# Gated gradient times w2 transposed made ahead of each chunk's MLP, w1 transposed kept on chip, third chunk turned on TensorE

## The chip, the cores and the metric

The kernel runs on one core of one Trainium2 chip. The metric is device time in microseconds (us) of one execution; the time of a kernel is the median of several executions. Of one execution there is also a hardware profile. Its engines are PE (TensorE, matrix products), PEld (the loads of PE's weights), DVE (VectorE), ACT (ScalarE), POOL (GpSimd) and SP (SyncE, which here only issues DMAs). Each engine works through its own instructions in the order in which the program wrote them; all engines run at once and wait for each other by semaphores. ACT and POOL issue some DMAs too, in the same order as their other instructions.

## The reference

The forward pass of one transformer block with adaptive layer norms, and the gradients of all its inputs. It is differentiated with `jax.vjp`, so the kernel computes both the output and nine gradients.

```python
mod = (silu(c) @ w_mod).reshape(1, 6, 1, 512)
sa, ca, ga, sb, cb, gb = (mod[:, i] for i in range(6))
h = layernorm(x) * (1 + ca) + sa
x = x + ga * attention(h, wqkv, wo)        # 32 heads of 16, 2048 tokens
h = layernorm(x) * (1 + cb) + sb
x = x + gb * (relu(h @ w1 + b1) ** 2 @ w2 + b2)   # 512 -> 1792 -> 512
```

For this change only the MLP's backward matters. With g the incoming gradient, gf = gb * g (the gated gradient), z = h @ w1 + b1, r = relu(z) and s = r * r, it needs ds = gf @ w2^T, then dz = 2 * r * ds, then dh = dz @ w1^T, and the weight gradients s^T @ gf (for w2) and h^T @ dz (for w1). All inputs and outputs are bf16.

## The kernel before

2048 tokens are four chunks of 512. The program has five stages, one after the other: a preparation (norms, first projections); the forward attention; the last chunk's MLP; the backward attention; and a tail.

**Forward attention.** 512 units of work, one for a chunk of queries (4), a group of four heads (8) and a tile of 128 keys (16). In each unit PE makes the scores of four heads (`psST`, L579), ACT takes their exponential in two instructions (`ET`, L581), and PE multiplies the result of two units earlier with the values (L595). The pool of `psST` has three buffers of two heads, so PE's scores can be up to one and a half units ahead of ACT.

**Dense work in the forward.** While the attention of chunk c+1 runs, the dense work of chunk c (the output projection, the second norm, the MLP forward and backward, the gradient up to the attention) is cut into steps, and `step` (L1128) puts one step into each unit. `dense_chunk` (L321) is a generator that yields after each step; `yield n` waits n units, `yield -2` runs one weight-gradient product ("chain", four products of 128 tokens each, `add_chain` L225) out of the queue `dwq`. All these steps use one PSUM bank (`pm`, one buffer), so a step's product waits until DVE has emptied the one before. `later(lag, ...)` puts an instruction, mostly a DMA on SP's queue, `lag` units later.

For one chunk, in order: O_c turned by a DMA transpose (L343), projection, norm, xn2 turned by a DMA transpose (L365), then 14 products z = w1^T h (L404, tile `wA`), each followed on DVE by the relu into `rT` (L406) and the square into `sT` (L407); then w2 transposed is loaded into the same buffer `wA` (L412), and 14 products ds (L418) follow, each multiplied on DVE by 2 r into dz (L421). Then dh (L444) with w1 transposed out of `wB`, which each chunk loads again from a copy in DRAM (`w1T_st`, L295); then the MLP's output (L500) and the attention gradient (`attn_grad`, L528). gf is made on POOL (L306) and turned by a DMA.

**The last chunk** cannot hide behind forward attention. `late_finish` (L659) and `last_chunk` (L1245) run it alone, on PE with all engines free for it. It loads w2 transposed and w1 transposed (L1529 to L1534), finishes the norm while PE runs chains left over from chunk 2 (`fill`, L1287 and L1295), and then has two loops of 14 iterations, each with a `tick` that issues what is due and then runs one chain:

- first loop (L1344): product z; relu on ACT (L1349); square on DVE (L1350); tick; `turn` of the s of the iteration before: four PE transposes (L1334) and a copy on ACT (L1335);
- second loop (L1359): product ds (L1362); dz on DVE straight out of PSUM (L1365); tick; `turn` of the dz of the iteration before.

A chain of the last chunk adds what earlier chunks left in DRAM: DVE adds `acc` and the fetched part (L236), and at the next tick ACT issues the DMA of the result (L237). Because ACT's queue is in order, ACT waits there until DVE has made the result. After the loops come dh (L1388), the layer-norm gradient, the attention gradient and the MLP's output (L1440), with the loads for the backward attention in between (`head_loads`; K as `KS_tok`, L1373; dOs as `dOs_tok`, L1475).

Of the kernel before, what the change touches and what calls it, by code (L numbers as in the profile page):

```python
# [13 lines left out]
dt = mybir.dt  # L14
# [6 lines left out]
P = 128  # L21
D = 512
DC = 4
# [11 lines left out]
def kernel(  # L35
# [64 lines left out]
    w1T_st = dram.tile([P, FC, D], BF, name="w1T_st")  # L100
# [45 lines left out]
    with ExitStack() as ph:  # L146
# [32 lines left out]
        def later(lag, f, *args):  # L179
            due.append((unit[0] + lag, f, args))  # L180

        def run_due(everything=False):
            i = 0
            while i < len(due):
                if everything or due[i][0] <= unit[0]:
                    _, f, args = due.pop(i)
                    f(*args)
                else:
                    i += 1
# [88 lines left out]
        def load_wB(src, lag, rate=1):  # L278
            w = ffw.tile([P, FC, D], BF, name="wB", tag="wB")
            for s in range(7):  # L280
                later(lag + int(s * rate), sp, w[:, 2 * s:2 * s + 2, :], src[:, 2 * s:2 * s + 2, :])
            return w

# [3 lines left out]
        begun = {}  # L287

        def chunk_loads(c):
            ts = slice(4 * c, 4 * c + 4)  # L290
            end = c == QC - 1
            if end:
                L = dict(begun)
            else:
                L = {"w1": load_wA(w1_src, 6), "w1T": load_wB(w1T_st[:], 20)}  # L295
                L["g"] = cb.tile([P, 4, D], BF, name="g_c", tag="g_c")
                sp(L["g"][:], g_dram[:, ts, :])
            L["wo"] = ffw.tile([P, DC, D], BF, name="wo_nat", tag="wo")
            sp(L["wo"][:], A_wo.rearrange("(oc p) j -> p oc j", p=P))
            L["x1"] = cb.tile([P, 4, D], BF, name="x1_c", tag="x1_c")  # L300
            sp(L["x1"][:], x_dram[:, ts, :])
            L["gf"] = cb.tile([P, 4, D], BF, name="gf_c", tag="gf")
            L["gfT"] = cb.tile([P, 4, DC, P], BF, name="gfT", tag="gfT")

            def scaled(ti):
                POOL.tensor_tensor(L["gf"][:, ti, :], L["g"][:, ti, :], gb_bc, ALU.mult)  # L306
                if ti < 3:
                    return
                later(3, sp, L["gfT"].rearrange("p t o q -> p (t o) q"), flat(L["gf"]), True)

            def sums(ti):
                rowsum(4, L["g"][:, ti, :], 4 * c + ti)

            if end:
                return L
            for ti in range(4):
                later(14 + ti, scaled, ti)
                later(27 + 2 * ti, sums, ti)
            return L

        def dense_chunk(c, O_c, L):  # L321
            ts = slice(4 * c, 4 * c + 4)
            g_c, x1_c, gf_c, gfT, w1_nat, w1T = (L[key] for key in ("g", "x1", "gf", "gfT", "w1", "w1T"))
# [19 lines left out]
            later(3, sp, OT.rearrange("p t o q -> p (t o) q"), flat(O_c), True)  # L343
            yield 6
# [11 lines left out]
            stats(2)  # L356
            stats(3)
# [5 lines left out]
            for ti in range(4):  # L363
                normed(ti)
            later(3, sp, h2T.rearrange("p t o q -> p (t o) q"), flat(xn2_c), True)  # L365
            yield 6
            while dwq and dwq[0][1] < c:
                yield -2
            for ic in range(DC):
# [12 lines left out]
            rT = cb.tile([P, FC, 512], BF, name="rT", tag="rT")  # L382
# [18 lines left out]
            for fc in range(FC):  # L401
# [4 lines left out]
                DVE.tensor_scalar(rT[:, fc, :], pz[:], b1col[:, fc:fc + 1], 0.0, ALU.add, ALU.max)  # L406
                DVE.tensor_tensor(sT[:, fc, :], rT[:, fc, :], rT[:, fc, :], ALU.mult)  # L407
# [4 lines left out]
            w2T = load_wA(w2T_st[:], 1)  # L412
            yield 3
            dzT = rT
            for fc in range(FC):
                pds = mm()
                for oc in range(DC):
                    PE.matmul(pds[:], w2T[:, oc, fc * P:(fc + 1) * P], gfT[:, :, oc, :],  # L418
                              start=(oc == 0), stop=(oc == DC - 1))
                db1p = wk.tile([P, 1], F32, name="db1p", tag="db1p")  # L420
                DVE.scalar_tensor_tensor(out=dzT[:, fc, :], in0=pds[:], scalar=2.0, in1=rT[:, fc, :],  # L421
                                         op0=ALU.mult, op1=ALU.mult, accum_out=db1p[:])
                POOL.tensor_tensor(db1acc[:, fc:fc + 1], db1acc[:, fc:fc + 1], db1p[:], ALU.add)
                yield 0
                if fc % 3 == 2 or fc == FC - 1:
                    f0 = fc // 3 * 3
                    while len(dwq) > FC - (fc + 1) + n_dz[0]:
                        yield -2
                    to_tokens("dz", dzT, f0, fc + 1)
            if c == QC - 2:  # L430
                begun["w1"] = load_wA(w1_src, 1)
            else:
                w2_nat = ffw.tile([P, FC, D], BF, name="w2_nat", tag="wA")
                for s in range(7):
                    later(1 + 3 * s, sp, w2_nat[:, 2 * s:2 * s + 2, :], w2_src[:, 2 * s:2 * s + 2, :])
# [4 lines left out]
            for ti in range(4):  # L440
                t = 4 * c + ti
                pdh = mm()
# [48 lines left out]
            if c == QC - 2:  # L491
                w2_nat = load_wB(w2_src, 1)
                yield 6
            else:
                yield 3
# [17 lines left out]
            later(2, sp, out0_v[:, ts, :], x1_c[:])  # L513
            if c == QC - 2:
                begun["g"] = cb.tile([P, 4, D], BF, name="g_c", tag="g_c")
                later(1, sp, begun["g"][:], g_dram[:, 4 * c + 4:4 * c + 8, :])
            dOs_c = cb.tile([P, 4, D], BF, name="dOs_c", tag="xn2_c")
            dOT = cb.tile([P, DC, 4, P], BF, name="dOT", tag="gfT")
# [114 lines left out]
        def early_finish():  # L633
# [8 lines left out]
            gf, gl = L["gf"], L["g"]  # L642
            for ti in range(4):
                later(1 + ti // 2, scale_heads, O_c, ou, ti, 4 * qc + ti, g)
                later(3 + ti // 2, DVE.tensor_tensor, gf[:, ti, :], gl[:, ti, :], gb_bc, ALU.mult)
# [33 lines left out]
        def ffinish(qc, rr, ou, L):  # L679
# [5 lines left out]
            for ti in range(4):  # L685
                scale_heads(O_c, ou, ti, qc * 4 + ti, HG)
            dense.append(dense_chunk(qc, O_c, L))
# [43 lines left out]
        def turn_weights(i):  # L731
            if i == 2:
                turned["1"] = ffw.tile([P, FC, D], BF, name="w1T_0", tag="wB")
                turned["2"] = ffw.tile([P, DC, FF], BF, name="w2T_0", tag="wA")
                turned["o"] = ffw.tile([P, DC, D], BF, name="woT_0", tag="wo")
            if 2 <= i < 6:
                for fc in range(4 * (i - 2), min(FC, 4 * (i - 2) + 4)):
                    sp(turned["1"][:, fc, :], B_w1[:, fc * P:(fc + 1) * P], True)
            if 7 <= i < 11:
                sp(turned["2"][:, i - 7, :], B_w2[:, (i - 7) * P:(i - 6) * P], True)  # L740
                sp(turned["o"][:, i - 7, :], A_wo[:, (i - 7) * P:(i - 6) * P], True)
            if i == 12:
                sp(w1T_st[:], turned["1"][:])
# [382 lines left out]
        loads = {}  # L1126

        def step(u):  # L1128
            nonlocal wait, turn
            ripe = dwq and not open_group[0] and u >= dwq[0][0]  # L1130
            if wait > 0 or not dense:
                wait = max(0, wait - 1)
                if ripe:
                    next_chain()
                return
            if ripe and turn and ((len(dwq) > 14 and fqueue) or dwq[0][3]):
# [5 lines left out]
            if w == -2:  # L1142
                next_chain()
            elif w == -1:
# [100 lines left out]
        def last_chunk(O_c, L, w1T, w2T):  # L1245
            c = QC - 1
            ts = slice(4 * c, 4 * c + 4)
            g_c, x1_c, gf_c, gfT, w1_nat = (L[key] for key in ("g", "x1", "gf", "gfT", "w1"))
# [26 lines left out]
            for half in range(2):  # L1275
# [20 lines left out]
                else:  # L1296
                    PE.matmul(pd[0:1, :], onesf[:, 0:1], racc[:, 4, :], start=True, stop=False)
                    for ti in range(4):
                        PE.matmul(pd[0:1, :], ones_bf[:, 0:1], g_c[:, ti, :], start=False, stop=(ti == 3))
# [18 lines left out]
            for i in range(6):  # L1318
                later(7 + i, fetch_part, FC + i)
# [3 lines left out]
            rT = cb.tile([P, FC, 512], BF, name="rT", tag="rT")  # L1323
# [20 lines left out]
            for fc in range(FC):  # L1344
# [4 lines left out]
                ACT.activation(rT[:, fc, :], pz[:], AF.Relu, bias=b1col[:, fc:fc + 1])  # L1349
                DVE.tensor_tensor(sT[:, fc, :], rT[:, fc, :], rT[:, fc, :], ALU.mult)  # L1350
# [3 lines left out]
            later(3, sp, woT[:], woT_st[:])  # L1354
            w2_nat = ffw.tile([P, FC, D], BF, name="w2_1", tag="wA")
            for s in range(7):
                later(5 + 2 * s, sp, w2_nat[:, 2 * s:2 * s + 2, :], w2_src[:, 2 * s:2 * s + 2, :])
            dzT = rT
            for fc in range(FC):  # L1359
                pds = mm()  # L1360
                for oc in range(DC):
                    PE.matmul(pds[:], w2T[:, oc, fc * P:(fc + 1) * P], gfT[:, :, oc, :],  # L1362
                              start=(oc == 0), stop=(oc == DC - 1))
                db1p = wk.tile([P, 1], F32, name="db1p", tag="db1p")
                DVE.scalar_tensor_tensor(out=dzT[:, fc, :], in0=pds[:], scalar=2.0, in1=rT[:, fc, :],  # L1365
                                         op0=ALU.mult, op1=ALU.mult, accum_out=db1p[:])
                POOL.tensor_tensor(db1acc[:, fc:fc + 1], db1acc[:, fc:fc + 1], db1p[:], ALU.add)
                if fc == 7:
                    head_loads()
                tick()  # L1370
                turn(*(("dz", dzT, fc - 1) if fc else ("s", sT, FC - 1)))
# [806 lines left out]
```

## Time and profile before

| | us |
|---|---|
| median of 3 runs (2461.6 to 2465.69) | 2463.31 |
| the profiled execution | 2460.92 |
| its span in the profile | 2459.1 |
| forward attention, from 38 to 984 us of the span | 946 |
| start of the last chunk, 984 to 1002.83 (norm; first z product at its end) | 18.8 |
| two loops of the last chunk, 1002.83 to 1055.85 | 53.0 |
| rest of the last chunk, 1055.85 to 1102.2 | 46.4 |
| backward attention, 1102.2 to about 2340 | 1238 |
| tail, to the end | 119 |

Over the whole span PE is busy 94%, DVE 74%, ACT 94%, POOL 21%. The boundaries of the stages were read from the order of instructions on PE: the last scores of the forward, the first z product, the first dh product and the first scores of the backward. A page line gives source line, engine, operation, what is written and read, a count, busy time and mean duration, and the idle time of the engine just before such instructions with what ended it. In a timeline, each row has a start, a duration, and in brackets the idle time before it.

### The profile page before, as it was taken

To read this page: it belongs to the slowest core of one execution; us is meant where nothing else is said; L and a number is where in the kernel's file an instruction comes from. 1 tells how busy PE (TensorE), PEld (TensorE's weight loads), DVE (VectorE), ACT (ScalarE), POOL (GpSimd) and SP (SyncE) were. 2 spreads that over 40 slices of the span, in tenths; PEclk is the share of its full clock that TensorE was granted. 3 is DMA by queue.
4 is the path that set the end of the run, shared out by engine and by line. 5 is a ranking of instruction groups with operands and counts; after the bars stand their busy time and mean duration, and the time that the engine had idled before them with its cause. 6 is when DMAs were issued, how large, how long until landed. Compare 5 with 4: busy or idle time off the path is not lost. (4 is left out here: it accounts for less than half of the span.)

```text
span 2459.1 us, 49701 instructions
## 1 busy us (share of the span) xinstructions
PE 2305.4 (94%) x18860; PEld 765.7 (31%) x18860; DVE 1825.8 (74%) x2361; ACT 2300.9 (94%) x3581; POOL 510.4 (21%) x692
## 2 busy tenths in 40 slices
PE   8899889988998999999999999999999999999999
PEld 3232223222322322442233233323233333233244
DVE  6555163455445554579999999999999999999885
ACT  8999999999999999639999999999999999999965
POOL 2111132423544352200111101111011010110112
PEclk9999999999999999999999999999999999999999
DMA  4478475267738866979999999999999999999997
GB/s 155 126 169 179 145 158 127 71 165 154 126 70 161 161 131 123 264 221 178 200 199 207 202 206 198 210 206 206 196 218 199 211 206 208 202 212 199 195 231 176
DMA packets 1217027, 440.81 MB, mean 179 GB/s; under 512 B 1093750, under 2 KB 1189620, under 8 KB 1216532
## 3 DMA queue, kind: packets, MB, share of 16 engines
q1 hardware_dynamic: 1171604, 381.60, 81.6%
q0 software_dynamic: 23472, 33.77, 8.0%
q10 hardware_dynamic: 21712, 22.27, 3.9%
q8 instruction: 148, 2.42, 0.4%
q14 instruction: 91, 0.75, 0.1%
HBM read 94.63 MB, written 70.78 MB: 67 GB/s over the span
## 5 line engine op out<-in xcount | busy, mean ns | idle before, releaser
L1656 DVE TENSOR_TENSOR dS_u<-psD_u,E_u 128x1024 bf16<-128x1024 f32 x1024 | 1185.3, 1216 | 68.1 <-PE psD_u L1654 27.3
L581 ACT ACTIVATE ET<-psST 128x1024 bf16<-128x1024 f32 x1024 | 942.1, 1309 | 5.4 <-PE psST L579 4.9
L1640 ACT ACTIVATE E_u<-psS_A 128x512 bf16<-128x512 f32 x768 | 513.0, 668 | 11.1 <-PE psS_C L1634 8.1
L1640 ACT ACTIVATE E_u<-psS_B 128x512 bf16<-128x512 f32 x768 | 506.0, 659 | 5.7 <-PE psD_u L1654 1.3
L1654 PE MATMUL psD_u<-iv,ido 32*128 32x512 bf16 x2048 | 408.5, 387 | 0.2
L579 PE MATMUL psST<-qt_sb,kt_sb 32*128 32x512 bf16 x2048 | 315.1, 385 | 50.3 <-ACT ET L581 46.7
L1640 ACT ACTIVATE E_u<-psS_C 128x512 bf16<-128x512 f32 x512 | 335.5, 655 | 4.6 <-DMA dsT<-dS_u 2.4
L1634 PE MATMUL psS_A<-ik,iq 32*128 32x512 bf16 x768 | 292.6, 381 | 10.8 <-DMA d_st<-dltT 0.9
L1634 PE MATMUL psS_B<-ik,iq 32*128 32x512 bf16 x768 | 294.3, 383 | 8.6 <-ACT E_u L1640 1.0
L1741 POOL TENSOR_TENSOR dQacc<-dQacc,dqtmp 128x512 f32<-128x512 f32 x64 | 81.2, 1269 | 847.4 <-ACT dqtmp L1736 785.4
L1634 PEld LDWEIGHTS <-iq 32*128 32x128 bf16 x2048 | 129.7, 91 | 315.1 <-issue 297.8
L1696 PE MATMUL accVK<-dS_u,qz 128*32 128x512 bf16 x2048 | 212.0, 388 | 0.4 <-PE psD_u L1654 0.3
L595 PE MATMUL oacc<-ET,vaug 128*32 128x512 bf16 x2048 | 207.4, 393 | 0.0
L1705 PE MATMUL accVK<-E_u,dOs_tok 128*16 128x512 bf16 x2048 | 202.9, 386 | 0.0
L1634 PE MATMUL psS_C<-ik,iq 32*128 32x512 bf16 x512 | 193.5, 378 | 4.5 <-ACT dqtmp L1736 0.2
L579 PEld LDWEIGHTS <-kt_sb 32*128 32x128 bf16 x2048 | 84.0, 91 | 334.7 <-issue 317.9
L1723 PE MATMUL dqacc<-dsT,KS_tok 128*32 128x512 bf16 x2048 | 146.2, 383 | 15.0 <-ACT E_u L1640 1.6
L250 DVE COPY part<-pm 128x512 f32<-128x512 f32 (+2 forms) x103 | 63.4, 616 | 118.5 <-PE pm L232 112.4
L1800 ACT ACTIVATE dsT<-ptT 128x1024 bf16<-128x1024 bf16 x126 | 143.6, 1140 | 6.1 <-PE ptT L1686 5.7
L1654 PEld LDWEIGHTS <-ido 32*128 32x128 bf16 x2048 | 104.3, 91 | 98.0 <-issue 92.1
L1696 PEld LDWEIGHTS <-qz 128*32 128x32 bf16 x2048 | 58.3, 94 | 177.5 <-issue 162.5
L1741 POOL TENSOR_TENSOR dQst<-dQacc,dqtmp 128x512 bf16<-128x512 f32 x32 | 40.6, 1269 | 266.2 <-ACT dqtmp L1736 266.2
(434 smaller groups left out, 2682.2 us busy)
## 6 DMA issues: line engine op xcount, KB each, us to landing
p_st<-part POOLq DMA_DIRECT2D x36, 256.0 KB, 4.9
kt_sb<-qkT_st POOLq DMA_DIRECT2D x124, 64.0 KB, 3.5
wA<-in_B_w_dram SPq DMA_DIRECT2D x28, 256.0 KB, 5.6
wB<-w1T_st SPq DMA_DIRECT2D x21, 256.0 KB, 3.4
wA<-w2T_st SPq DMA_DIRECT2D x21, 256.0 KB, 5.1
p_st<-part POOLq DMA_DIRECT2D x25, 192.0 KB, 5.5
p_st<-part SPq DMA_DIRECT2D x18, 256.0 KB, 2.1
part<-p_st SPq DMA_DIRECT2D x18, 256.0 KB, 3.9
```

Of the source, the lines that this page charges most:

```text
L579: PE.matmul(ps[:, hi, :], kt_sb[r:r + 32, kt * P:(kt + 1) * P], qt_sb[r:r + 32, :], start=True, stop=True, tile_position=(r, 0))
L581: ACT.activation(ET[:, 2 * pair:2 * pair + 2, :], ps[:], AF.Exp, scale=SCALE)
L595: PE.matmul(oacc[32 * hq:32 * hq + 32, :], lhsT, ET[:, hq, :], start=(kt == 0), stop=(kt == TT - 1), tile_position=(0, 32 * hq), skip_grou ...
L1634: PE.matmul(psS[:], st["q"][r:r + 32, qt * P:(qt + 1) * P], st["k"][r:r + 32, kc * 512:kc * 512 + 512], start=True, stop=True, tile_positi ...
L1640: ACT.activation(bst[u][0][:, hq, :], sst.pop((u, hq))[:], AF.Exp, scale=SCALE)
L1654: PE.matmul(psD[:, hi, :], st["do"][r:r + 32, qt * P:(qt + 1) * P], st["v"][r:r + 32, kc * 512:kc * 512 + 512], start=True, stop=True, til ...
L1656: DVE.tensor_tensor(dS_u[:, 2 * pair:2 * pair + 2, :], psD[:], E_u[:, 2 * pair:2 * pair + 2, :], ALU.mult)
L1696: PE.matmul(cur["vk"][32 * hq:32 * hq + 32, :], hst[hg]["qz"][:, qt, hq, :], bst[u][1][:, hq, :], start=(qt == 0), stop=False, tile_positi ...
L1705: PE.matmul(acc[32 * hq:32 * hq + DH, :], dOs_tok[:, qt, (hg * 4 + hq) * DH:(hg * 4 + hq + 1) * DH], E_u[:, hq, :], start=False, stop=(qt ...
L1723: PE.matmul(acc[32 * hq:32 * hq + 32, :], KS_tok[:, kc * 4 + kt, h * DH:h * DH + 32], tT[:, :, hq * 4 + kt, :], start=(kt == 0), stop=(kt ...
L1741: POOL.tensor_tensor(dst2, dst, tmp[:], ALU.add)
L1800: ACT.activation(dst, pt[:], AF.Identity)
```

## The change

- ds is made ahead. `gate(c)` loads g, makes gf (on DVE now) and turns it, loads w2 transposed into the buffer of `sT` and w1 into `wA`, and queues 14 ds products in `dsq`. Each is copied by DVE to a bf16 tile (`dsT`, in the buffer of `rT`). `step` runs them where there is no dense step, or alternating with chains; `dense_chunk` runs those that are left before its z loop. `gate(c + 1)` is called in chunk c after the MLP's output.
- So the z loop makes relu, square and dz in one go, with r in a small tile and dz from `dsT`; the second loop is gone, in the forward and in the last chunk. The last chunk's ds is made during the forward's end.
- The chains of dz are queued during the dh steps, not before them.
- w1 transposed stays in `wB` from the preparation to the last chunk: its DRAM copy and its loads are gone, in the last chunk those of w2 transposed too.
- Chunk 2 (the third) turns O_c and xn2 by PE transposes and DVE copies, not by DMA.
- The buffer for the last chunk's chain results and fetched parts (`dwbuf`) moves from `wB` to the place where K for the backward is loaded later, so those loads come later, after all chains of the loop.
- The column sum of g of the last chunk is on POOL in the forward, not four PE products.
- When no dense work is left, up to 8 chains are held back for the last chunk.

```diff
+        def spaced(lag, f, *args):
+            due.append((unit[0] + lag, f, args, False))
...
+        def gate(c):
+            G["g"] = cb.tile([P, 4, D], BF, name="g_c", tag="g_c")
+            sp(G["g"][:], g_dram[:, ts, :])
...
+                G["w2T"] = cb.tile([P, DC, FF], BF, name="w2T", tag="sT")
+                for s in range(7):
+                    b = slice(256 * s, 256 * s + 256)
+                    spaced(6 + s // 2, sp, G["w2T"][:, :, b], w2T_st[:, :, b])
+            G["w1"] = ffw.tile([P, DC, FF], BF, name="wA", tag="wA")
...
+            def scaled(ti):
+                DVE.tensor_tensor(G["gf"][:, ti, :], G["g"][:, ti, :], gb_bc, ALU.mult)
+                if ti == 3:
+                    spaced(2, sp, G["gfT"].rearrange("p t o q -> p (t o) q"), flat(G["gf"]), True)
...
+            def product(fc):
+                if fc == 0:
+                    G["ds"] = cb.tile([P, FC, 512], BF, name="dsT", tag="rT")
+                pds = mm()
+                for oc in range(DC):
+                    PE.matmul(pds[:], G["w2T"][:, oc, fc * P:(fc + 1) * P], G["gfT"][:, :, oc, :],
+                              start=(oc == 0), stop=(oc == DC - 1))
+                DVE.tensor_copy(G["ds"][:, fc, :], pds[:])
+            for ti in range(4):
+                spaced(3 + ti, scaled, ti)
+                spaced(14 + 2 * ti, sums, ti)
+            for fc in range(FC):
+                dsq.append((unit[0] + 13, c, product, fc))
...
+            on_pe = c == QC - 2
...
+            while dsq and dsq[0][1] == c:
+                yield -3
+            dzT = L["ds"]
...
-                DVE.tensor_scalar(rT[:, fc, :], pz[:], b1col[:, fc:fc + 1], 0.0, ALU.add, ALU.max)
-                DVE.tensor_tensor(sT[:, fc, :], rT[:, fc, :], rT[:, fc, :], ALU.mult)
+                r = wk.tile([P, 512], BF, name="rz", tag="ta")
+                DVE.tensor_scalar(r[:], pz[:], b1col[:, fc:fc + 1], 0.0, ALU.add, ALU.max)
+                DVE.tensor_tensor(sT[:, fc, :], r[:], r[:], ALU.mult)
+                db1p = wk.tile([P, 1], F32, name="db1p", tag="db1p")
+                DVE.scalar_tensor_tensor(out=dzT[:, fc, :], in0=dzT[:, fc, :], scalar=2.0, in1=r[:],
+                                         op0=ALU.mult, op1=ALU.mult, accum_out=db1p[:])
...
-            later(2, sp, out0_v[:, ts, :], x1_c[:])
+            sp(out0_v[:, ts, :], x1_c[:])
+            gate(c + 1)
...
@@ last_chunk
-                ACT.activation(rT[:, fc, :], pz[:], AF.Relu, bias=b1col[:, fc:fc + 1])
-                DVE.tensor_tensor(sT[:, fc, :], rT[:, fc, :], rT[:, fc, :], ALU.mult)
+                r = wk.tile([P, 512], BF, name="rz", tag="ta")
+                ACT.activation(r[:], pz[:], AF.Relu, bias=b1col[:, fc:fc + 1])
+                DVE.tensor_tensor(sT[:, fc, :], r[:], r[:], ALU.mult)
+                DVE.scalar_tensor_tensor(out=dzT[:, fc, :], in0=dzT[:, fc, :], scalar=2.0, in1=r[:],
+                                         op0=ALU.mult, op1=ALU.mult, accum_out=db1p[:])
...
                 tick()
                 if fc > 0:
                     turn("s", sT, fc - 1)
+                    tick()
+                    turn("dz", dzT, fc - 1)
+            turn("s", sT, FC - 1)
+            tick()
+            turn("dz", dzT, FC - 1)
...
-            for fc in range(FC):
-                pds = mm()
-                for oc in range(DC):
-                    PE.matmul(pds[:], w2T[:, oc, fc * P:(fc + 1) * P], gfT[:, :, oc, :],
-                              start=(oc == 0), stop=(oc == DC - 1))
...
-                turn(*(("dz", dzT, fc - 1) if fc else ("s", sT, FC - 1)))
...
+            fill(len(dwq))
+            later(2, ks_loads)
             mlp(0, {5: lambda: finish_dx(3), 7: lambda: turn_da(2), 11: lambda: grad(1)})
```

## The prediction

> **What bounds the kernel now.** First I read the busy time of each engine by stage, cut at the first instructions of each stage on PE (columns: stretch, its length, busy time and count of PE, PEld, DVE, ACT, POOL, granted clock, DMA share, GB/s).
>
> ```profile
> 38.00:984.00 946.00, 858.24 (x5935) 273.89 (x5932) 463.23 (x905) 940.56 (x1023) 311.35 (x491) 0.99 0.63 138
> 984.00:1002.83 18.83, 14.59 (x91) 6.54 (x90) 13.12 (x33) 12.00 (x22) 7.79 (x9) 1.00 0.97 232
> 1002.83:1055.85 53.02, 52.75 (x336) 28.52 (x336) 30.25 (x69) 28.26 (x48) 6.89 (x19) 0.97 1.00 276
> 1055.85:1102.20 46.35, 45.42 (x232) 19.61 (x230) 36.13 (x81) 13.39 (x28) 0.31 (x1) 1.00 0.80 217
> ```
>
> The forward (first row) is ACT's: 940.56 of 946 us. The last chunk's two loops (third row) are PE's: 52.75 of 53.02, with DVE and ACT half idle. So work taken from PE counts in the loops only, and work given to PE or DVE in the forward is free until it makes ACT wait. The waits say how often that happens now: 4.9 us in all.
>
> ```profile
> ACT ET L581 <- PE psST L579: 4.9, 15, 0.9
> ```
>
> Next, PE's timeline in the two loops: one iteration of the first, one of the second. The reader should take the distance from row to row (the durations overlap).
>
> ```profile
> 1028.13 1.03 PE L1347 MATMUL pm<-h2T,wA 128*128 128x512 bf16 x4
> 1029.00 1.03 PE L232 MATMUL pc<-gf_c,tk 128*128 128x512 bf16 x4
> 1029.86 0.39 PE L1334 MATMUL ptk<-identb,sT 128*128 128x128 bf16 x4
> 1030.08 1.03 PE L1362 MATMUL pm<-gfT,w2T 128*128 128x512 bf16 x4
> ...
> 1051.12 0.81 PE L232 MATMUL pc<-tk,h_c 128*128 128x384 bf16 x4
> 1051.77 0.39 PE L1334 MATMUL ptk<-identb,rT 128*128 128x128 bf16 x4
> ```
>
> Four products of 512 columns take 0.87 us, a chain of 384 columns 0.65 (1051.12 to 1051.77), four transposes 0.22; a chain of 256 columns 0.43 (same view, 1007.30 to 1007.74). No row of these has idle time.
>
> **What is removed.** The 14 ds products of the last chunk: 14 x 0.87 = 12.1 us of PE. Of the chains left from chunk 2, the changed instruction order keeps six (two of 384, four of 256) where there were eleven (seven and four); the five that ran in the first loop are gone: 0.65 + 4 x 0.43 = 2.4 us. Were PE still the bound, the loops would fall by 14.5. The four column sums of g (0.87) and the shorter chains before the loops (6 x 0.65 = 3.9 becomes 3.0) stand in the second row's stage, where PE then waits 1.41 us for DVE's xn2 anyway: nothing.
>
> **What the new loop costs.** Its order on ACT is relu, result DMA, copy of s, result DMA, copy of dz; on DVE square, dz, result, result; on PE z, chain, turn s, chain, turn dz. These rows of before give the links:
>
> ```profile
> 1019.45 0.69 ACT L1349 ACTIVATE rT<-pm,b1col 128x512 bf16<-128x512 f32 x1 [0.27 <-PE pm L1347]
> ...
> 1020.17 0.43 DVE L1350 TENSOR_TENSOR sT<-rT 128x512 bf16<-128x512 bf16 x1 [0.70 <-ACT rT L1349]
> ...
> 1020.48 0.34 ACTq L187 DMA_DIRECT2D out_dram<-dwbuf  x1
> 1020.51 0.68 DVE L236 TENSOR_TENSOR dwbuf<-pc,part 128x512 bf16<-128x512 f32 x1
> 1020.87 0.60 ACT L1335 ACTIVATE tk<-ptk 128x512 bf16<-128x512 bf16 x1 [0.73 <-DVE sT L1350]
> ...
> 1021.40 0.69 ACT L1349 ACTIVATE rT<-pm,b1col 128x512 bf16<-128x512 f32 x1
> ```
>
> Relu to square 0.72, square to next DVE work 0.34, a result 0.68 (0.55 with 384 columns), a DMA on which ACT had waited to the next copy 0.39, that copy to the next relu 0.53. Now ACT's second DMA waits for a result that stands on DVE behind square and dz of the same relu, and the copy of dz and the next relu stand on ACT behind that DMA. That is a ring: 0.72 + 0.34 + dz + 0.68 + 0.05 + 0.39 + 0.53. dz out of SBUF isn't in the trace: at least 0.62 (L1365, 1047.91 to 1048.53, out of PSUM), at most 0.78 (L1419, all in SBUF, 1064.08 to 1064.86); I take 0.70, nearer the second, which reads SBUF too. The ring takes 3.4 us with a 512 chain and 3.3 with a 384 one. PE's own work in an iteration is 0.87 + 2 x 0.22 + two chains = 2.6 to 3.0. So ACT and DVE, not PE, now set the pace. In the old first loop the DMA waited for a result of the iteration before; no ring.
>
> Sum of the new loop. First z with its wait for h2T (0.65 + 0.20 idle as before) and second z begun: 1.9. Iterations 1 to 3: the queue is empty, so the chain just turned must run at once: z 0.87, 0.20 to ACT, relu 0.58, copy 0.60, 0.05, chain 0.87, turn 0.22 = 3.4 each, 10.2. Iterations 4 to 13, ten: between PE's 2.8 and the ring's 3.3, slack in the first, 3.2 each: 32. Closing (turn, copy, chain, turn): 2.2. That is 46.3. Two additions: half clock for 2.7 us as now (rows below), 1.3; and ACT's waits at DMAs, of which before shows 0.73, 0.93 and 1.23 in 28 iterations: I take 1.0 in all. 48.6 against 53.0: 4.4 less. In the dh part 7 x 0.65 + 4 x 0.43 becomes 4 x 0.65 + 2 x 0.87 + 4 x 0.43: 0.2 less. Gain 4.6.
>
> **Clock.** A stretch in which PE was busy 4.60 of 6.80 us is followed by half clock, and so is one of 2.94 of 4.30:
>
> ```profile
> 996.00:1002.80 6.80, 4.60 (x31) 1.97 (x29) 5.17 (x16) 4.23 (x10) 4.16 (x5) 1.00 1.01 288
> ...
> 1004.30:1007.00 2.70, 2.70 (x9) 1.13 (x8) 0.42 (x1) 1.18 (x2) 0.00 (x0) 0.52 1.13 268
> ...
> 1102.00:1106.30 4.30, 2.94 (x15) 0.92 (x15) 2.43 (x3) 3.21 (x7) 3.98 (x3) 0.95 0.48 155
> 1106.30:1116.20 9.90, 9.49 (x52) 1.69 (x51) 7.13 (x6) 6.46 (x12) 4.81 (x3) 0.50 0.53 97
> ```
>
> The new iterations 1 to 3 use 2.2 of 3.4 us, 64%, like those stretches; half clock as long as the second (9.9 us) would cost up to 5 us, as PE loses half of what it would have done. I charge only the 2.7 us already there. The Trainium skill (TensorE: Matmul & The Clock Gate, Part 1: The HAM clock gate) says that the clock halves after an idle window of about 3.4 us; no single idle of the loop is so long, so by that rule not even the 1.3 would be charged and the time would be 1.3 lower, but the rows above halve with no idle over 1.41, and the rows decide.
>
> **What is added to the forward,** at 0. Per chunk 14 copies of ds on DVE (0.69, L250 of that shape), 4 products of gf (0.42; 1.17 on POOL before); in chunk 2, 32 PE transposes (1.7 us) and four copies near 0.7 (L654 has 0.56 for 768 columns). All 14 ds of the last chunk are issued by unit 506 of 512. DVE has 463 of 946; the cover is PE's lead over ACT of 1.5 units of 1.85 us, 2.8 us. Tightest is DVE in the z steps: relu 0.78, square 0.35, dz 0.62 to 0.78 and its sum 0.08, so 1.83 to 1.99 a unit, seven in a row: at most 1 us behind, 1.7 with the copy of `ostage` (0.68). Before, POOL's sums of g stretched the squares there to 1.4 and PE's steps to 2.1 without one wait of ACT; those sums move to units without squares. Without cover each us costs one. Bounds: a gain of 4.9 (all waits gone) to the loss of the last rival.
>
> The profiled execution had 2460.9 (span 2459.1 and 1.8 around it), 2.4 under the median of 2463.3. 2460.9 - 4.6 = 2456.3; at the median 2458.7.
>
> **Rivals.**
>
> PE stays the bound in iterations 4 to 13 (ACT's DMAs wait less than I think): 14 x 0.87 + 28 x 0.22 + 12 chains of 0.87 and 12 of 0.65 = 36.6, 0.9 for h2T, 3 x 1.2 early idle, 1.3 clock: 42.4, gain 10.8. For it: DVE and ACT are busy 2.4 and 2 us of 3. Against: the ring. 2452.5.
>
> The loop gives it all back: ACT's DMAs wait another 0.5 in each of ten iterations (8.3 MB in 30 us at 278 GB/s are already near the most seen, 405), or the half clock lasts. Loop 53, gain 0: 2463.
>
> Slower: in the forward, ds of the next chunk is not ready. `gate` stands in unit 228; the first ds in unit 241, 24 us later, on an in-order PE with the scores behind it. In between: SP stores the output, loads g (landing 4.0 to 7.4 us), DVE, which also empties PE's one bank, multiplies from unit 231, the DMA transpose of gf (5.07 us for this shape at 977.78) is due in unit 236, so done about 20 us after the gate, and the last piece of w2T stands behind it on SP's queue, landing 4 to 5 us later, at 24 to 25. With 2.8 us of lead that just fits; it decides from 3 us more. SP's queue has some 25 DMAs in those units, several waiting for DVE. 5 us beyond, at three gates: +15, so 2463.3 - 4.6 + 15 = 2474.
>
> **Chances.** Forecast 0.50 (own range 2455 to 2462), PE-bound 0.20, given back 0.17, slower 0.13. A difference of 0.2% (4.9 us) is about what a measurement of this kernel tells from none; faster means under 2458.4. The forecast lies on that line: half of it counts as faster, with the PE-bound case 0.45; slower (over 2468.2) 0.15 with the tails; the rest 0.40. Range 2450 to 2469: it leaves out the worst of the slower case and a PE-bound loop with less forward wait.
>
> **What would show it.** Right: iterations of the new loop of 3.2 to 3.4 us with PE idle before chains or turns and ACT waiting at result DMAs; ACT's waits in the forward still near 5 us; the loop 47 to 50. Wrong: iterations of 2.6 to 3.0 without PE idle (PE-bound), a clock near 0.5 over ten us in the loop, or `psST` waits of some us at the first ds of a chunk. Also wrong if the later load of `KS_tok`, with the `dOs_tok` loads around it, makes the backward start late; there it has about 15 us until dQ needs it.

## The result, and the profile after

| | median | runs | ratio to before, 95% interval |
|---|---|---|---|
| before | 2466.37 us | 20 | |
| changed | 2477.65 us | 20 | 1.0041 [1.0026, 1.0055] |

The change makes the kernel slower, by 0.41%. 2458.7 was forecast, with a range up to 2469. Some 3 us of the distance are the base: the forecast was reckoned from a median of 2463.3 of three runs, and the kernel before has 2466.4 here.

The stages, cut on PE at the first score of the forward, its last score, the first z of the last chunk, its first dh and the first backward score; each kernel has two profiles, the second from the runs told of below:

| us | before | before, again | changed | changed, again |
|---|---|---|---|---|
| forward | 945.3 | 946.4 | 957.9 | 955.3 |
| last chunk up to z | 21.1 | 21.2 | 21.4 | 21.2 |
| loop(s) | 53.0 | 53.2 | 47.5 | 45.9 |
| rest of the last chunk | 46.4 | 46.4 | 46.1 | 46.1 |
| backward and tail | 1356.9 | 1359.9 | 1367.8 | 1373.3 |

The same in the busy time by stage of the changed kernel (columns as in the prediction):

```profile
36.60:994.50 957.90, 868.42 (x5993) 280.15 (x5993) 481.81 (x982) 940.09 (x1024) 305.61 (x487) 0.99 0.61 129
994.50:1015.92 21.42, 15.15 (x100) 7.38 (x100) 13.85 (x35) 13.64 (x24) 8.64 (x10) 0.96 0.78 130
1015.92:1063.45 47.53, 42.35 (x264) 22.34 (x264) 28.12 (x69) 24.53 (x41) 2.67 (x14) 0.91 0.69 194
1063.45:1109.51 46.06, 45.20 (x228) 19.20 (x225) 36.66 (x81) 14.03 (x29) 0.31 (x1) 1.00 0.91 266
```

The loop did what was forecast of it. The forward did not: ACT has the same 1024 exponentials and the same 940 us of work as before, but the stage is 12.6 us longer. The waits of the changed kernel name what ACT stood for:

```profile
ACT ET L617 <- PE psST L615: 17.1, 19, 6.1
```

17.1 us where there were 4.9, and one wait alone has 6.1. Here it is, in the timeline of the changed kernel, in chunk 0 (start, duration, engine, line, operation; in brackets the idle time before it and what ended it):

```profile
311.87 0.39 DVE L350 TENSOR_TENSOR atmp<-a_c,modbc 128x512 bf16<-128x512 bf16 x1
311.92 1.04 PE L318 MATMUL pm<-gfT,w2T 128*128 128x512 bf16 x4
...
314.38 0.17 DVE L119 TENSOR_SCALAR rsq<-mv 128x4 f32<-128x4 f32 x1
...
317.35 1.38 DVE L360 TENSOR_SCALAR xn_c<-x_c,mv,rstd 128x512 bf16<-128x512 bf16 x4
318.65 0.69 DVE L320 CAST dsT<-pm 128x512 bf16<-128x512 f32 x1
319.39 1.86 PE L318 MATMUL pm<-gfT,w2T 128*128 128x512 bf16 x4 [5.56 <-DVE dsT L320]
321.18 0.61 PE L615 MATMUL psST<-qt_sb,kt_sb 32*128 32x512 bf16 x4
...
321.89 1.02 ACT L617 ACTIVATE ET<-psST 128x1024 bf16<-128x1024 f32 x1 [6.08 <-PE psST L615]
```

Read it from the bottom. ACT waits for scores. The scores stand on PE behind the next ds product, which waits 5.56 us for the forward's only bank for such products (`pm`). The bank is freed by the copy of the ds product before it. That product was done at 313.0; but its copy stands on DVE behind the rest of the chunk's layer norm, which was all issued in one unit ahead of it: the last input, two statistics, 16 steps of the reciprocal root at 0.2 us, four `xn_c`, until 318.65. Before the change PE had no product for this bank in these units, so the same block hurt nobody.

PE's pause costs twice. The clock of the changed kernel, in the stretch behind it:

```profile
316.00:319.00 3.00, 0.00 (x0) 0.00 (x0) 2.76 (x12) 0.00 (x0) 0.00 (x0) 0.81 0.00 0
319.00:326.00 7.00, 6.61 (x32) 1.64 (x31) 1.72 (x3) 3.14 (x4) 0.00 (x0) 0.59 0.40 75
```

The next ds product takes 1.86 us instead of 1.04, and ACT waits once more, 0.97 us at 324.8: 7.05 us for this one place. The Trainium skill (TensorE: Matmul & The Clock Gate, Part 1: The HAM clock gate) says that a window of about 3.4 us without work halves the clock; the trace agrees here, with a pause of 5.56 us and 6.8 us of half clock from 317.8 on. Half clock comes without such a pause too: the clock is 0.51 from 959.6 to 963.0, where the pause before it was 1.78 us.

A second wait, of 1.90 and 0.56 us, is at the first ds product of the last chunk. SP's queue and PE there, in the changed kernel:

```profile
948.46 6.19 SPq L176 DMA_TRANSPOSE gfT<-gf_c  x1
...
956.02 0.58 SPq L176 DMA_DIRECT2D w2T<-w2T_st  x1
...
959.10 1.46 PE L318 MATMUL pm<-gfT,w2T 128*128 128x512 bf16 x4 [1.78 <-DMA dOT<-dOs_c]
```

The last piece of w2T stands on SP behind the transposition of gf, as the prediction's slower case had it, and PE starts 3 us after its issue. Which of the two DMAs PE waits for isn't shown: the releaser is named after another DMA of the same queue. The other waits that the kernel before did not have are of 0.2 to 0.6 us each, at units where a chain's or ds's copy, `ostage` (0.69) and the three steps of z meet on DVE, and where gf's products fall between those of the attention gradient.

The loop of the changed kernel, one iteration on ACT and DVE:

```profile
1052.08 0.42 DVE L1394 TENSOR_TENSOR sT<-rz 128x512 bf16<-128x512 bf16 x1 [1.04 <-ACT rz L1393]
1052.42 0.69 DVE L1396 SCALAR_TENSOR_TENSOR dsT<-dsT,rz 128x512 bf16<-128x512 bf16 x1
...
1053.03 1.28 DVE L238 TENSOR_TENSOR dwbuf<-pc,part 128x512 bf16<-128x512 f32 x2
...
1053.75 0.36 ACTq L189 DMA_DIRECT2D out_dram<-dwbuf  x1
...
1054.15 0.60 ACT L1378 ACTIVATE tk<-ptk 128x512 bf16<-128x512 bf16 x1 [1.62 <-DVE dwbuf L238]
1054.35 0.34 ACTq L189 DMA_DIRECT2D out_dram<-dwbuf  x1
1054.65 0.68 ACT L1393 ACTIVATE rz<-pm,b1col 128x512 bf16<-128x512 f32 x1
```

This is the forecast ring: square, dz, result on DVE, then the result's DMA on ACT, and behind it the copy, for which ACT was idle 1.62 us, and the next relu.

What is left is the end. The chain of waits of the changed kernel has, in the tail, a row that the first profile of before has not:

```profile
2440.75 18.65 DMA KS_tok<-ido
2459.39 0.14 issue
2459.53 3.61 PE pwx L2058 x16
```

A transposition lands 18.65 us after its issue, and PE, which had other work until then, waits 2.39 us for it. No instruction of the backward or the tail was changed; the further profiles below come back to this.

### The profile page after: what moved, and what is told of

It is laid out like the page before. It is cut to its first block, busy times and chain, and to the rows that moved or that the text cites. A ratio compares the mean times of both kernels' runs of the same rounds, so it can differ in the third digit from the quotient of the medians.

```text
span 2477.3 us, 49619 instructions
## 1 busy us (share of the span) xinstructions
PE 2309.1 (93%) x18844; PEld 766.3 (31%) x18844; DVE 1844.0 (74%) x2438; ACT 2298.5 (93%) x3576; POOL 501.4 (20%) x684
## 5 line engine op out<-in xcount | busy, mean ns | idle before, releaser
L617 ACT ACTIVATE ET<-psST 128x1024 bf16<-128x1024 f32 x1024 | 942.3, 1297 | 17.8 <-PE psST L615 17.1
L1678 ACT ACTIVATE E_u<-psS_A 128x512 bf16<-128x512 f32 x768 | 509.6, 664 | 11.3 <-PE psS_C L1672 8.0
```

The costliest lines, as they stand in the source:

```text
L617: ACT.activation(ET[:, 2 * pair:2 * pair + 2, :], ps[:], AF.Exp, scale=SCALE)
L1678: ACT.activation(bst[u][0][:, hq, :], sst.pop((u, hq))[:], AF.Exp, scale=SCALE)
```

## The experiments

**The ds products kept out of the layer norm.**

```diff
                 for ti in range(4):
                     normed(ti)
+                ln_until[0] = unit[0] + 5
                 later(3, sp, h2T.rearrange("p t o q -> p (t o) q"), flat(xn2_c), True)
...
-                ready = dsq and not open_group[0] and u >= dsq[0][0]
+                ready = dsq and not open_group[0] and u >= max(dsq[0][0], ln_until[0])
```

> The changed kernel, but in chunk 0 the four ds products that stood in the units behind the layer norm's block on DVE (two with_input, three stats, 16 small steps of rsqrt of 0.2 us each, four normed of 0.35) are held for five units and run a few units later. Theory A (the copy of each ds stands on DVE behind that block, the next ds and the scores behind it on PE, so ACT waits 6.08 + 0.97 us at 321.9 and 324.8): these two waits vanish, ACT's waits for scores fall from 17.1 to about 10 us, the forward from 957.9 to 951, the time by 7, to about 2470 against 2477.7. Theory B (DVE or PE has simply too much work around there, or the half clock of 6.8 us that lies on this place is the cause and comes anyway): the wait comes back some units later, ACT's waits stay at 15 to 17 us, the time at 2477.

Counted by the score products in the traces, the four products of units 149 to 152 run in units 153 to 158, the next one in unit 159, and chunk 0 ends two units later; from unit 270 on the order is the same. Measured: median 2465.43 (12 runs), ratio to before 0.9996 [0.9975, 1.0017]. The forward takes 951.2 us, and its waits are:

```profile
ACT ET L619 <- PE psST L617: 11.3, 19, 2.6
```

Both waits at 322 are gone, and the clock is 1.00 from 306 to 326 us: theory A, to the microsecond in the forward. No wait of that size came instead, but the small ones between 330 and 540 us add up to 2.4 us where the changed kernel had 0.9, so ACT's waits are 11.3 and not 10. The median fell by 9 to 12 and the mean by 8.6, not by 7; the difference is within what 12 runs tell (standard error of their mean 1.9).

**The block cut instead.** The ds products stay in the layer norm's units, and the block is issued in three portions.

```diff
-            if on_pe:
-                yield 1
+            yield 1
             stats(3)
...
             else:
+                yield 1
                 for ti in range(4):
                     normed(ti)
-                later(3, sp, h2T.rearrange("p t o q -> p (t o) q"), flat(xn2_c), True)
-                yield 6
+                later(2, sp, h2T.rearrange("p t o q -> p (t o) q"), flat(xn2_c), True)
+                yield 5
```

> The changed kernel with the ds products left in the units of the layer norm, but the block on DVE cut in three: with_input and two stats; one unit later the third stats and the 16 steps of rsqrt (3.2 us); two units later the four normed (1.4). Theory A (ds waits for as much of the block as stands ahead of its copy on DVE): the wait of 6.08 + 0.97 at 322 us falls to at most 1.5, as rsqrt with 3.2 us is little over PE's lead of 2.8; the half clock of 6.8 us behind it goes; ACT's waits 10 to 12 us, forward 951 to 953, time 2465 to 2470. Rival (the place is what matters, not the length of the block; a ds product in a unit of the layer norm always stalls): a wait of 4 us or more stays and the time is 2473 or more.

Ratio 1.0019 [1.0, 1.0037], median 2469.06, forward 953.1. No wait at all at 322: length, not place, as far as this goes; the cut also spreads the ds products, to units 149, 151 and 153. But the later order brought another wait of 4.19 us in chunk 1, again through DVE's queue, in this kernel's timeline:

```profile
502.71 0.56 DVE L252 COPY part<-pm 128x384 f32<-128x384 f32 x1 [5.02 <-DMA p_st<-part]
503.33 1.86 PE L318 MATMUL pm<-gfT,w2T 128*128 128x512 bf16 x4 [3.67 <-DVE part L252]
```

Here the copy waits for a free `part` buffer, whose store stands on SP's queue. The bank is held by whatever its copy waits for.

**Both kernels again.**

> The changed kernel once more, for a second profile and a time on this chip. Theory A: what the two profiles of before and after showed in the forward (12.2 us more of ACT waiting, 12.8 longer) comes again within 1 us, as it follows from the order of the instructions; the tail's 18.65 us of waiting for a transposition into KS_tok does not, or is as likely before, as no instruction there was changed. Rival: the change makes the tail worse, and the wait comes again.

Ratio 1.0039 [1.0018, 1.006], median 2474.48. ACT's waits are 15.0 us, with 6.09 and 0.82 at the same place; the last chunk's first ds doesn't hold ACT up this time. So the forward came again only within 2.6 us, not within 1: the long stall follows from the order of the instructions, the wait at the last chunk's first ds does not. The transposition into `KS_tok` is on the chain again, with 16.6 us, but PE's wait for it is under 0.8 us, and the tail is 3 us shorter than in the first profile; over all the profiles here this wait is 2.39, 1.98, 1.11 and, in the other eight, under 0.8. The backward, though, from its first to its last score of `psS_A`, takes 1261.5 us, against 1253.0 in the first profile and 1249.0 and 1250.1 before.

> The kernel before once more, for a second profile: forward 945 us from first to last score within 1 us, ACT's waits for scores near 4.9 us, loops 53 us. What differs by more than that between two profiles of one kernel (backward and tail 1356.9 us in the first) is not the change's.

Forward 946.4 and waits 5.9, each 1 us over the first profile; backward and tail 3.0 us longer than in the first profile.

**All results of the loop on SP.**

```diff
-                    later(1, sp if late else ACT.dma_start, dst, res)
+                    later(1, sp, dst, res)
```

> The changed kernel, but the results of the last chunk's chains are issued on SP, not on ACT: ACT no longer waits at them. Theory A (the ring relu, square, dz, result, DMA on ACT, copy sets the pace of the later iterations): the loop from the first z to the first dh falls from 47.5 us to 42 to 45, its iterations to the 2.6 to 3.0 of PE. Rival: SP holds the loads of the parts behind the results, which then come late, and PE or DVE waits for them: the loop stays at 47 or grows. The forward doesn't change.

The loop falls to 42.1 us, its iterations to PE's own 2.6 to 3.0. The z products of the last four iterations, first in the changed kernel, 3.1 to 3.2 us apart, then in this one:

```profile
1048.37 1.02 PE L1390 MATMUL pm<-h2T,wA 128*128 128x512 bf16 x4
1051.57 1.03 PE L1390 MATMUL pm<-h2T,wA 128*128 128x512 bf16 x4
1054.80 1.02 PE L1390 MATMUL pm<-h2T,wA 128*128 128x512 bf16 x4
1057.93 1.02 PE L1390 MATMUL pm<-h2T,wA 128*128 128x512 bf16 x4
...
1044.29 1.03 PE L1390 MATMUL pm<-h2T,wA 128*128 128x512 bf16 x4
1047.33 1.03 PE L1390 MATMUL pm<-h2T,wA 128*128 128x512 bf16 x4
1049.93 1.03 PE L1390 MATMUL pm<-h2T,wA 128*128 128x512 bf16 x4
1052.55 1.03 PE L1390 MATMUL pm<-h2T,wA 128*128 128x512 bf16 x4
```

But the rest of the last chunk grows from 46.1 to 51.0, and the time stays: ratio 1.0037 [1.0016, 1.0058], median 2476.83. Its waits say why; SP holds the results back, and DVE has no buffer for the next:

```profile
DVE dwbuf L238 <- DMA out_dram<-dwbuf: 8.0, 8, 2.7
```

Both theories were half right: the ring set the pace, and SP could not take all of it.

**One result of two on SP,** on the kernel with the held ds products.

```diff
-                    later(1, sp if late else ACT.dma_start, dst, res)
+                    later(1, sp if late or ring[0] else ACT.dma_start, dst, res)
...
+                ring[0] = True
                 tick()
+                ring[0] = False
```

> The kernel of the held ds products, with only one of the two results of an iteration moved from ACT to SP: the one that DVE makes behind square and dz of the same relu, whose issue stands on ACT ahead of the copy of dz. Theory A (the ring is closed by this one DMA): the loop falls as with both moved, from 45.9 to 42 to 43 us, and as SP has half as many results, the rest of the last chunk stays nearer 46 than the 51.0 it took with both; the time falls by up to 3 us. Rival (any result on ACT holds the copies up): the loop stays at 45 to 46.

Loop 42.2, rest 46.4: one DMA closed the ring. Median 2462.25, ratio 0.9997 [0.998, 1.0015]. The stages up to the backward take 1058.2 us, 6.0 less than in the kernel it is built on: 3.7 in the loop, and most of the others because ACT waits 0.99 us at the last chunk's first ds and not 2.63. The median is 3 lower, but so is, by 1.8, that of the kernel before beside it: the runs can't tell the gain from none; the loop's own time can.

**w2T ahead of gf,** on the kernel with the held ds products.

```diff
-                    spaced(6 + s // 2, sp, G["w2T"][:, :, b], w2T_st[:, :, b])
+                    spaced(4 + s // 2, sp, G["w2T"][:, :, b], w2T_st[:, :, b])
```

> The kernel of the held ds products, with the pieces of w2T issued two units earlier after each gate, so that they stand on SP ahead of the transposition of gf (6.19 us there) and not behind it. Theory A (the wait at about 960 us, 1.9 + 0.56, 2.63, 1.36 and none in four profiles, is PE waiting for the last piece of w2T, which lands 3 us after SP got free of that transposition): no wait there, ACT's waits for scores 11.5 to about 9 us, the forward 951 to 949. Rival (the transposition of gf itself, or SP's other work, is what comes late): a wait of 1 to 3 us stays at the first ds of the last chunk. The time falls by at most 2 us, which this measurement hardly tells.

Median 2463.8, ratio 1.0 [0.9981, 1.002]. The wait is 0.89 us, not none: now gf's transposition is last on SP, and PE waits for it, as it does in the kernel with all parts below:

```profile
946.02 4.23 SPq L177 DMA_TRANSPOSE gfT<-gf_c  x1
955.66 1.86 PE L320 MATMUL pm<-gfT,w2T 128*128 128x512 bf16 x4 [3.43 <-DMA gfT<-gf_c]
```

Here it stands 9.6 us after the issue. With w2T late the wait was 2.46 (both parts), 2.63, 1.36, 0.99, 0.99 and none, with w2T early 0.89, 3.95 and, with gf on POOL, none. The DMAs between gate and first ds just fit, and how late the last lands varies from run to run. So the transposition of gf can be late by itself, and moving w2T was not the cure.

**All together, with gf on POOL.**

```diff
-                DVE.tensor_tensor(G["gf"][:, ti, :], G["g"][:, ti, :], gb_bc, ALU.mult)
+                POOL.tensor_tensor(G["gf"][:, ti, :], G["g"][:, ti, :], gb_bc, ALU.mult)
```

> All together: held ds products, w2T earlier, one result of two on SP, and the product gf of the gate on POOL (1.17 us each there) as before the change, not on DVE, where its copies fall between those of the attention gradient (ACT waits of 0.48, 0.22, 0.60 and 0.23 us at 711, 715, 938 and 946). Theory A (all waits add up): ACT's waits for scores 7 to 8 us, the forward 948, the loop 43, the time 2459 to 2463, 0.1 to 0.3% under the kernel before. Rival (POOL makes gf too late for its transposition, or SP is too full): the first ds of a chunk waits several us, and the time is 2467 or more.

The rival's outcome, though not for its reason: median 2467.2, ratio 1.0003 [0.9987, 1.0019], ACT's waits 15.7 us, of which 2.41, 2.53 and 2.56 (2.00 and 0.56) are new, at the gates. The timeline of this kernel at the first of them:

```profile
472.30 3.38 POOL L308 TENSOR_TENSOR gf_c<-g_c,modbc 128x512 bf16<-128x512 bf16 x3
472.76 2.96 DVE L583 TENSOR_SCALAR dlt<-delta 128x32 bf16<-128x32 f32 x1
...
475.64 0.54 DVE L253 COPY part<-pm 128x384 f32<-128x384 f32 x1
476.24 1.02 PE L571 MATMUL pm<-woT,daT 128*128 128x512 bf16 x4 [2.94 <-DVE part L253]
...
477.69 1.02 ACT L620 ACTIVATE ET<-psST 128x1024 bf16<-128x1024 f32 x1 [2.41 <-PE psST L618]
```

A DVE instruction of 32 columns, 0.18 us elsewhere, takes 2.96: it ends when POOL's three products end.

**All together, gf left on DVE.**

> Held ds products, one result of two on SP, w2T two units earlier, gf on DVE as in the change: the parts that won in the stages (forward 948.0, loop 42.1, rest 46.5), without gf on POOL, which lost. Theory A (what the stages gain adds up): from the first score to the first backward score 1058 us, against 1066 in the two profiles of the kernel before and 1073 and 1068 of the changed one; the median 2458 to 2463, 0.1 to 0.3% under before. Rival (a gain there is given back in the backward or the tail by the clock, as the 2462 of the kernel without the earlier w2T suggests, which had 1058 too): the same 1058, but a median of 2462 to 2465, no difference from before that can be measured.

Median 2462.4 (12 runs), ratio to before 0.9979 [0.996, 0.9998]: under the kernel before, barely, and some 14 us under the changed one (means 2462.0 and 2475.8). The stages up to the backward took 1063.3 in its profile, not the 1058 that both theories expected, mostly because of the 3.95 us that ACT waited for gf; loop 42.1, rest 46.7. The median lies where the two theories' ranges overlap, so it doesn't decide between them.

## Why the prediction was wrong

**The step that failed** is "What is added to the forward, at 0". It named PE's lead of 2.8 us as the cover, and tested the cover against DVE's work in the z steps, as the tightest place. The cover was mis-sized, and the place was the wrong one.

*The cover* is about 0.5 us, not 2.8. In the forward attention of all eleven profiles, from 100 us on, PE stands 15 times for over 1.2 us before a product of four matmuls (ds or dense work). At full clock ACT's wait behind it is 0.44 to 0.54 shorter than PE's (1.90 to 1.36, 1.42 to 0.89, 2.94 to 2.41); where the pause is followed by half clock, it is 0.52 to 0.53 longer (2.10 to 2.63, 3.43 to 3.95, 5.56 to 6.08); the one case between lies between (1.78 to 1.90). One of the pauses at full clock, in the kernel with one result of two on SP:

```profile
951.20 1.02 PE L320 MATMUL pm<-gfT,w2T 128*128 128x512 bf16 x4 [1.53 <-DMA dOT<-dOs_c]
...
952.64 1.02 ACT L620 ACTIVATE ET<-psST 128x1024 bf16<-128x1024 f32 x1 [0.99 <-PE psST L618]
```

Three buffers say how far PE can be ahead of ACT, not how late it may begin the next product, as that product and the scores still have to be made. The trace of before showed this already. The prediction says that PE's steps of 2.1 us in the z steps came "without one wait of ACT"; there is one of 0.16 to 0.19 us at four steps of chunk 1 and at four of chunk 2, 1.4 of the 4.9 us:

```profile
574.16 1.02 PE L404 MATMUL pm<-h2T,wA 128*128 128x512 bf16 x4 [0.44 <-DVE rT L406]
...
575.61 1.94 ACT L581 ACTIVATE ET<-psST 128x1024 bf16<-128x1024 f32 x2 [0.17 <-PE psST L579]
...
576.28 1.02 PE L404 MATMUL pm<-h2T,wA 128*128 128x512 bf16 x4 [0.44 <-DVE rT L406]
...
577.73 1.94 ACT L581 ACTIVATE ET<-psST 128x1024 bf16<-128x1024 f32 x2 [0.18 <-PE psST L579]
```

With 2.8 us of cover the long stall would have cost some 3.6 us (5.56, and 0.8 for the product at half clock, less 2.8) and not 7.05, and the last chunk's first ds nothing.

*The place.* The test was a sum of work per unit, and it was asked of the wrong units. What matters for a product on a single bank is how much stands on DVE ahead of its copy when it is issued. Ds products go where PE has nothing else; one such place is just behind the chunk's layer norm, where DVE has over 6 us in its queue. The trace of before had it all: the block is there, with the same operations. The step names the added operations and their durations, but not what stands ahead of each in its queue. Cutting or avoiding the block removed the 7 us; the other 3 to 5 are small pile-ups and the last gate.

**The z steps** were costed at up to 1.7 us of lateness, judged covered. They gave waits of 0.33 to 0.54 us at five places where `ostage` or a chain's copy joined them, some 2 us in all, and the eight small waits of before went. The place was seen; the cover was not there.

**The slower rival** had the right sign, and its time of 2474 stands near the result, but not by its mechanism. It priced late DMAs at 5 us for each of three gates. They cost ACT 0 to 4 us at the last gate and nothing at the first ds of the other two, so it is luck that its time came near. The chance of 0.15 for slower was too low because only this one way was considered in which ds could hold PE up, and that with a cover of 2.8.

**The loop** was right: ring forecast and found, 48.6 forecast, 47.5 and 45.9 measured. Iterations 4 to 13 were put at 3.2 each and take 3.0 on average (1030.63 to 1057.93 for nine): the first three and one more run at PE's own 2.6 to 3.0, and the ring sets the pace in the other five, 3.13 to 3.71. Half clock was charged with 2.7 us; it was 8.5 in the first profile's loop and 3.4 in the second's, enough for the 1.7 us between them. With the ring opened the loop takes 42.1 to 42.2: the prediction's case of a loop bound by PE had 42.4. The rest of the last chunk gained 0.3 where 0.2 was forecast.

**The account.** The changes up to the backward are, as means of the two profiles each, +10.8 for the forward, -6.4 for the loop and -0.2 for the other two rows: +4.2. All runs together (32 of the changed kernel, 82 of the kernel before) have means of 2475.8 and 2466.1, 9.7 apart, so some 5.5 us lie in the backward and tail. That the change causes them isn't shown. Backward and tail take from 1355.9 to 1373.3 us over the profiles, also among kernels without the stall, in stretches of half clock at other places each time, and in waits of 1 to 3 us for DMAs in the tail, such as the one for `KS_tok`. Against chance speaks that the mean granted clock of all runs is 0.983 for the three kernels that keep ds products unheld behind the layer norm, all with a stall of over 4 us in chunk 0 or 1 (0.9832 for the changed one), and 0.986 for the others (0.9858 before, 0.9856 to 0.9859 for five kernels with the ds products held, one of which has a stall of 3.95 at the last gate). Over 81 runs of the kernel before, the time goes with the clock, by 1.55 us per 0.001 (correlation -0.88); by that the lower clock goes with some 4 of the 9.7 us. Why a stall in the forward should lower the clock of the backward stays open. Nor do the stages add up without a stall: the held kernels with w2T ahead and with one result of two on SP have 5.4 and 8.2 us less up to the backward than the kernel before, but their mean times differ from it by +1.2 and -0.9. Some 7 us are given back behind the stages there, as far as one profile each can say, and why isn't shown either.

## What to carry to other kernels

Before a product is put into "free" time of PE, read what stands on the engine that empties its bank at the moment of issue: on an in-order queue with one bank, the longest block ahead of the copy is the price, not the copy's 0.7 us and not the engine's share of busy time. Read the cover from the waits that the trace already has, not from the number of buffers: here 0.5 us and not 2.8. Work moved off a bound stage helps only as far as the next ring; find that ring by following one buffer around all the engines that touch it, and open it at the one instruction that closes it, since moving everything (all results to SP) just moved the wait.

## What was not expected of the hardware

POOL held DVE up: `dlt`, with one operand in SBUF, took 2.96 us instead of 0.18, and `prodo`, with two, 2.06 and 2.47 instead of 0.42, at the other gates. The Trainium skill (SBUF — State Buffer, Who interferes with whom) says that the two engines share a pair of ports as an exclusive lock; the traces agree in that DVE stood while POOL worked, and `dlt` ended only when three POOL instructions in a row, some 1.16 us each, had ended. Before the change the same products ran on POOL too, but in units without the attention gradient's steps. There they held up the layer norm: `atmp` took 3.60 us instead of 0.41 at 308.0, and no product of PE waited for it.
